# Scoring by halves of tokens in one loop, x1's rows behind up, and down's last 64 rows loaded early

## The chip, the cores and the metric

The kernel runs on one NeuronCore of a Trainium2 chip. The metric is device time of one execution in microseconds, lower is better.

## The reference

One decode step (one token, width D = 640) of a transformer block with adaptive layer norm. All tensors are bf16.

```python
mod = silu(c) @ w_mod                       # 640 -> 6 x 640: sa, ca, ga, sb, cb, gb
h = layernorm(x) * (1 + ca) + sa
q = h @ wq                                  # 32 heads of 128
scores = q . k_cache * 128 ** -0.5          # k_cache, v_cache: [32, 16384, 128]
o = softmax(scores) @ v_cache               # per head
x = x + ga * (o @ wo)                       # wo: 4096 x 640
h = layernorm(x) * (1 + cb) + sb
x = x + gb * ((silu(h @ w_gate) * (h @ w_up)) @ w_down)   # 640 -> 1728 -> 640
```

There are 32 key and value heads for 32 query heads, so each cached row is used once. K and V together are 268 MB, the weights some 22 MB; all of it is read in one execution.

## The kernel before

**Pairs.** The 32 heads are handled in NP = 16 pairs. A pair's K lies in one of two slots of `kring` as [128 partitions, 256 tokens, 128 elements]: partitions 0 to 63 hold one head, 64 to 127 the other, and each partition has 256 tokens, 64 KB. V goes to the one buffer `vbuf` in the same shape, V of the last pair to slot 0 of `kring`. Before the pairs these buffers hold `w_mod` and `wq`, after them `wo` (in `vbuf`) and the MLP's weights (in slot 1).

**Score of a pair.** DVE multiplies K by the query in place and adds halves of the element axis onto each other ("folds"); TensorE (PE) sums the 16 elements that are left by 16 matmuls with an identity into `S_ps`. This is done in two parts per pair. In the loop `score(p, c)` takes a half of the elements for all 256 tokens: one multiplication (L554), two folds (L559, L564), and `reduce_mm` (L544) adds its 16 matmuls of 256 columns to the same sum; the two parts together give the 16 + 16 elements. For the first and the last pair `score_end(p, c)` takes all 128 elements of a half of the tokens (128): one multiplication (L570), three folds (L576), and `reduce_end` (L584) runs 16 matmuls of 128 columns.

**Softmax and PV.** `largest(p)` takes the largest score (DVE, L590), spreads it on a diagonal (ACT, `d2`, L592) and shares it over the partitions by a matmul (L594). `weigh(p)` takes the least over the row (DVE, L598) and makes the exponentials (ACT, L602). `pv(p)` is 64 matmuls of 512 columns (L518) and a copy by ACT (`acc`, L524); `diag(p)` picks the wanted blocks by eight matmuls (L533) and a copy by ACT (`ot`, L537).

**Order.** Every engine runs its own list in the order in which the Python code calls `op`; an operation waits on semaphores of the operations in `deps` on other engines. `step(p)` calls: score part 0 of p (with `largest(p-1)` and `weigh(p-1)` between its steps), reduction, `pv(p-1)`, score part 1, reduction, `diag(p-1)`. `plan.in_loop` turns the pairs into a hardware loop: PE from pair 1 to 14, one pair per turn; ACT and DVE from pair FIRST = 3 to 14, two pairs per turn. Addresses and the values waited for are then computed from the turn. SP's list, the DMA issues, is written out. The last pair (PL = 15) stands behind the loops in an order of its own: first part, `pv(14)`, `diag(14)`, second part, then `largest(15)` and `weigh(15)`.

**DMA.** SP issues K of pair p+1 when the last reduction of pair p-1 is done, V of pair p when `pv(p-1)` is done, `wo` after `pv(14)`, and after the last reduction `w_gate`, `w_up` and five pieces of `w_down`. All run in the one queue of SP. Only c and x are loaded from ACT's queue.

**Tail.** After `pv(15)` and `diag(15)`: `on`, `z`, `am`, `as` (normalizing, and bringing the output vector into columns), the projection (L684), `wo_row` and `wo_cols` (L690, L696), x1 (L706), the second layer norm, `gate0` and `gate` (L721), `x1_rows` (L743: x1 spread to four strips of rows by eight matmuls), `up` (L721), the SiLU steps on DVE and ACT (L750 to L755), `gu` (L756), and `down` (L773), where each of the four strips of 32 partitions makes a quarter of the 640 outputs. 1728 is 13 x 128 + 64: gate and up take the last 64 columns in a 14th chunk that overlaps the 13th by 64. Their down rows are loaded as 128 half rows of 640 B, so a matmul with `twice` (L757) doubles each value onto two partitions, and `gu_half` (L759) masks by parity.

The lines that the change touches, from the kernel:

Of the kernel before, what the change touches and what calls it, by code (L numbers as in the profile page):

```python
# [218 lines left out]
def build(nc, A_x, A_k, A_v, A_wq, A_wo, B_wg, B_wu, B_wd, c_in, w_mod, out):  # L219
# [15 lines left out]
    DOWN = [(0, 0, 4), (1, 0, 4), (2, 0, 4), (None, 0, 0), (3, 0, 1)]  # L235
    FCH = NF + 1
    QW = 32
    QR = 16
    RW = D // 4
    FIRST = 3  # L240

    es = ExitStack()
    with es:
# [20 lines left out]
        wt_v = kb[:, wd0 + NF * D:wd0 + NF * D + D // 2]  # L264
# [15 lines left out]
        rows = qbc[0:1].rearrange("p a d -> p (a d)")[:, 0:2 * D].rearrange("p (j n) -> p j n", j=2)  # L280
# [33 lines left out]
        gu_half = sb("gu_half", [128, 2], BF16)  # L314
        even = sb("even", [128, 2], F32)
        twice = sb("twice", [128, 64, 2], BF16)
# [3 lines left out]
        x1_sp = acc_sb[:, 0:RW]  # L320
        q_f = qbc[:].rearrange("p a d -> p (a d)")
# [32 lines left out]
        d_c = dma(rows[:, 0, :], c_in, "c", name="dma_c", eng="act")  # L354
        d_x = dma(rows[:, 1, :], A_x[0], "x", name="dma_x", eng="act")
# [18 lines left out]
        def f_cx(e):  # L374
            last = None
            for j in range(2):
                for k in range(KC):
                    last = e.matmul(cx_ps[:, j * KC + k:j * KC + k + 1], lhsT=rows[0:1, j, k:D:KC],
                                    rhs=ones_bf[0:1, 0:1], start=True, stop=True)
            return last  # L380
        o_cx = op(PE, f_cx, deps=[d_c, d_x, o_onesb], name="cx_col")
        o_cc = op(ACT, lambda e: e.activation(out=c_col[:], in_=cx_ps[:, 0:KC], func=ACTF.Copy), deps=[o_cx], name="c_f32")
        o_ec = op(ACT, lambda e: e.activation(out=ec[:], in_=c_col[:], func=ACTF.Exp, scale=-1.0), deps=[o_cc], name="ec")
        o_xf = op(ACT, lambda e: e.activation(out=x_f32[:], in_=cx_ps[:, KC:2 * KC], func=ACTF.Copy, accum_out=st[:, 0:1]), deps=[o_cx], name="x_f32")
# [35 lines left out]
        def f_e32(e):  # L420
# [3 lines left out]
        o_even = op(DVE, lambda e: e.tensor_reduce(  # L424
            out=even[:], in_=ident[:].rearrange("p (j k) -> p k j", k=2), axis=AX.X, op=ALU.add), deps=[o_ident], name="even")
        o_twice = op(DVE, lambda e: e.tensor_copy(out=twice[64:128], in_=ident[64:128, 64:128].unsqueeze(2).broadcast_to([64, 64, 2])), deps=[o_ident], name="twice")
# [44 lines left out]
        for g in range(H // 4):  # L471
            b = g % 2

            def f_q(e, g=g, b=b):
                last = None
                for k in range(KC):
                    last = e.matmul(q_ps[b][:, 0:512], lhsT=h_col[:, k:k + 1].broadcast_to([128, 128]),  # L477
                                    rhs=wq_v[:, k, g * 512:(g + 1) * 512], start=(k == 0), stop=(k == KC - 1))
                return last
# [8 lines left out]
            o_qev.append(ev)  # L488

# [50 lines left out]
        def reduce_mm(p, c, fold):  # L540
            def f_R(e):
                last = None
                for d in range(QW * c, QW * c + QR):
                    last = e.matmul(S_ps[:, 0:T2], lhsT=ident[:], rhs=kring[:, bass.ds(plan.slot(p), 1), :, d].rearrange("p o t -> p (o t)"),  # L544
                                    start=(d == 0), stop=(d == QW + QR - 1))
                return last
            return op(PE, f_R, deps=[fold, o_ident, o_exp[p - 1], o_gb, o_m1], name="R%d_%d" % (p, c))

        def score(p, c, between=None):

            kv4 = kring[:, p % 2].rearrange("p t (a d) -> p t a d", a=2)[:, :, :, QW * c:QW * c + QW]
            def f_mult(e):
                q4 = qbc[:, bass.ds(plan.at(p), 1), :].rearrange("p o (a d) -> p o a d", a=2)[:, :, :, QW * c:QW * c + QW].broadcast_to([128, T2, 2, QW])
                return e.tensor_tensor(out=kv4, in0=kv4, in1=q4, op=ALU.mult)  # L554
            o_m = op(DVE, f_mult,
                     deps=[d_k[p][-1]] + o_qev[p // 2], name="mult%d_%d" % (p, c))
            if between:
                between[0]()
            o_f = op(DVE, lambda e: e.tensor_tensor(out=kv4[:, :, 0], in0=kv4[:, :, 0], in1=kv4[:, :, 1], op=ALU.add),  # L559
                     deps=[o_m], name="fold%d_%d" % (p, c))  # L560
            if between:
                between[1]()
            lo = kv4[:, :, 0]
            return op(DVE, lambda e: e.tensor_tensor(out=lo[:, :, 0:QR], in0=lo[:, :, 0:QR], in1=lo[:, :, QR:QW], op=ALU.add),  # L564
                      deps=[o_f], name="fold%d_%db" % (p, c))

        def score_end(p, c, between=None):

            kv = kring[:, p % 2, KCUT[c]:KCUT[c + 1]]
            o = op(DVE, lambda e: e.tensor_tensor(  # L570
                out=kv, in0=kv, in1=qbc[:, p, :].unsqueeze(1).broadcast_to([128, KCUT[c + 1] - KCUT[c], 128]), op=ALU.mult),
                deps=[d_k[p][min(c, len(d_k[p]) - 1)]] + o_qev[p // 2], name="mult%d_%d" % (p, c))
            for i, w in enumerate((64, 32, 16)):
                if between and i < 2:
                    between[i]()
                o = op(DVE, lambda e, w=w: e.tensor_tensor(out=kv[:, :, 0:w], in0=kv[:, :, 0:w], in1=kv[:, :, w:2 * w], op=ALU.add),  # L576
                       deps=[o], name="fold%d_%d_%d" % (p, c, w))
            return o

        def reduce_end(p, c, fold):  # L580
            def f_R(e):
                last = None
                for d in range(16):
                    last = e.matmul(S_ps[:, KCUT[c]:KCUT[c + 1]], lhsT=ident[:], rhs=kring[:, p % 2, KCUT[c]:KCUT[c + 1], d],  # L584
                                    start=(d == 0), stop=(d == 15))
                return last
            return op(PE, f_R, deps=[fold, o_ident, o_exp[p - 1] if p else o_gb], name="R%d_%d" % (p, c))
# [22 lines left out]
        def step(p):  # L610
            reduce_mm(p, 0, score(p, 0, before(p)))
            pv(p - 1)
            o_R[p] = reduce_mm(p, 1, score(p, 1))
            diag(p - 1)

# [3 lines left out]
        reduce_end(0, 0, score_end(0, 0))  # L619
        o_R[0] = reduce_end(0, 1, score_end(0, 1))  # L620
        NLOOP = NP - 2
        for p in range(1, NP - 1):
            plan.in_loop(("pe",), "pairs", p - 1, NLOOP)
            if p >= FIRST:
                plan.in_loop(("act", "dve"), "pairs", (p - FIRST) // 2, (NP - 1 - FIRST) // 2)
            load_k(p + 1)
            step(p)
            load_v(p)
        plan.out_of_loop(("pe", "act", "dve"))

        PL = NP - 1
        load_v(PL)
        f0 = score_end(PL, 0, before(PL))
        reduce_end(PL, 0, f0)
        pv(PL - 1)
# [3 lines left out]
        diag(PL - 1)  # L641
        f1 = score_end(PL, 1)
        o_R[PL] = reduce_end(PL, 1, f1)
# [10 lines left out]
        for i, (b, r0, r1) in enumerate(DOWN):  # L654
            if b is None:
                dst, src = wt_v, B_wd[NF * 128:F, :].rearrange("q (h n) -> (q h) n", h=2)
            else:
                f0, n, j0 = BLOCKS[b]
                dst, src = wd_v[:, j0 + r0:j0 + r1, :], B_wd[f0:f0 + 128 * n, :].rearrange("(p r) n -> p r n", r=n)[:, r0:r1, :]
# [12 lines left out]
            in1=on_f[:].unsqueeze(2).broadcast_to([128, H, 4]), op=ALU.mult), deps=[o_on, o_msk], name="z")  # L672
        o_am = op(PE, lambda e: e.matmul(A_ps[:, 0:H], lhsT=Z[:], rhs=e32[:], start=True, stop=True),
# [14 lines left out]
        for c in range(len(WCUT) - 1):  # L688
            o_p = project(c)
        o_wr = [op(ACT, lambda e, a=a, b=b, ps=ps: e.activation(out=wo_row[:, a:b], in_=ps[:, 0:b - a], func=ACTF.Copy),  # L690
                   deps=[o_p, f1], name="wo_row%d" % a) for ps, a, b in ((wr_ps[0], 0, 512), (wr_ps[1], 512, D))]
# [18 lines left out]
        def chunk(j):  # L710
            if j == NF:

                return slice(F - 128, F)
# [3 lines left out]
        def f_gu(e, wv, ps_t, src, n, k0, k1):  # L717
            last = None
            for k in range(k0, k1):
                for j in range(FCH):  # L720
                    last = e.matmul(ps_t[:, n * j:n * j + n], lhsT=wv[:, k, chunk(j)], rhs=src[:, n * k:n * k + n],  # L721
                                    start=(k == 0 and j == 0), stop=(k == KC - 1 and j == FCH - 1), skip_group_check=True)
# [17 lines left out]
        def f_xr(e):  # L740
            last = None
            for r in range(4):
                last = e.matmul(xr_ps[32 * r:32 * r + 32, 0:RW], lhsT=wide(msk[:, r:r + 1]), rhs=x1_sp, start=True, stop=True,  # L743
                                tile_position=(0, 32 * r))
            return last
        o_xr = op(PE, f_xr, deps=[o_xsp, o_ot[PL], o_msk], name="x1_rows")
        o_x1r = op(ACT, lambda e: e.activation(out=x1_row, in_=xr_ps[:, 0:RW], func=ACTF.Copy), deps=[o_xr], name="x1_row")
# [83 lines left out]
```

## Time and profile before

| What | us |
|---|---|
| median of 3 runs | 680.36 |
| the runs | 680.29, 680.36, 680.75 |
| the profiled execution's own time | 680.16 |
| its span, first to last instruction | 678.4 |
| DVE busy in it | 512.9 (76%) |
| PE busy in it | 362.4 (53%) |
| ACT busy in it | 46.8 (7%) |
| bytes read | 290.47 MB, 428 GB/s over the span |

The profile is of one execution, and its times count from the span's first instruction. PE is TensorE's matmul part and PEld its weight loads, DVE VectorE, ACT ScalarE, SP SyncE. A row of the chain of waits is "start, duration, what"; a row of the timeline is "start, duration, engine, line, operation, tiles, count" and, in brackets, how long the engine sat idle before it and what ended that. A row of windows has the stretch, its length, the busy time of PE, PEld, DVE, ACT and POOL with the number of instructions, the granted clock of PE as a share of full speed, the DMA engines' busy share and GB/s.

### The profile page before, as it was taken

The page shows a single profiled execution, that of the slowest core. Times are in us where ns is not written, and L with a number is a line of the kernel's source. Part 1 is how long each engine was busy: PE and PEld are TensorE (multiplying, and loading weights), DVE is VectorE, ACT ScalarE, POOL GpSimd, SP SyncE. Part 2 cuts the span into 40 slices and gives each one's busy share as a digit, 9 for nine tenths or more (in the row PEclk, how much of TensorE's full clock was granted, in tenths as well). Part 3 has the DMA queues.
Part 4 walks back from the last instruction along what each step waited for, and adds up shares of the span by engine and source line. Part 5 has one row for each costly group of instructions (what it writes and reads, how often), then busy time and mean ns, then how long its engine had stood idle before and what let it go on. Part 6 is the DMA issues. An engine that isn't in the chain of part 4 may idle for free.

```text
span 678.4 us, 5422 instructions
## 1 busy us (share of the span) xinstructions
PE 362.4 (53%) x2075; PEld 145.4 (21%) x2076; DVE 512.9 (76%) x184; ACT 46.8 (7%) x147; POOL 0.7 (0%) x6
## 2 busy tenths in 40 slices
PE   2522275755628174654818365572817465481677
PEld 1101122221212122221302122121212222130236
DVE  2189997959596996959597795959698695959802
ACT  1110000100000000000000010000000000000011
POOL 0000000000000000000000000000000000000000
PEclk9965565565756565565657565565757555575666
DMA  9999999999999999999999999999999999999997
GB/s 374 439 459 437 433 433 430 429 429 433 433 433 433 433 433 437 433 433 433 433 433 433 437 433 433 433 433 433 433 433 433 433 433 433 433 433 433 430 409 305
DMA packets 6355, 290.58 MB, mean 428 GB/s; under 512 B 714, under 2 KB 972, under 8 KB 1484
## 3 DMA queue, kind: packets, MB, share of 16 engines
q1 hardware_dynamic: 6340, 290.48, 99.2%
q8 instruction: 5, 0.08, 0.0%
q14 instruction: 2, 0.02, 0.0%
q10 hardware_dynamic: 8, 0.00, 0.0%
HBM read 290.47 MB, written 0.00 MB: 428 GB/s over the span
## 4 chain that ended last, share of the span: by engine, by line
DMA 43%; DVE 30%; issue 13%; PE 13%; ACT 1%; DVEq 0%; SPq 0%
DMA kring<-in_A_k_cache_dram 40%; DVE kring L554 10%; PE psb L544 7%; DVE kring L559 6%; DVE kring L570 5%; DVE kring L576 5%; DMA vbuf<-in_A_wq_dram 4%; DVE kring L564 3%; PE psb L477 1%; PE psb L518 1%; PE psb L721 1%; PE psb L684 1%; PE psb L584 1%; PE psb L696 0%; DVE pm L590 0%
## 5 line engine op out<-in xcount | busy, mean ns | idle before, releaser
L554 DVE TENSOR_TENSOR kring<-kring,qbc 128x16384 bf16<-128x16384 bf16 x28 | 243.3, 8688 | 96.2 <-DMA kring<-in_A_k_cache_dram 96.2
L544 PE MATMUL psb<-kring,ident 128*128 x448 | 197.5, 607 | 122.4 <-DVE kring L564 122.4
L559 DVE TENSOR_TENSOR kring<-kring 128x8192 bf16<-128x8192 bf16 x28 | 123.8, 4421 | 0.5
L544 PEld LDWEIGHTS psb<-kring,ident 128*128 128x128 bf16 x448 | 53.9, 120 | 250.2 <-issue 249.3
L518 PE MATMUL psb<-vbuf,PZ 128*8 128x512 bf16 x960 | 79.9, 506 | 0.0
L594 PE MATMUL psb<-d,bd_f 128*128 128x64 f32 x32 | 11.0, 446 | 122.0 <-ACT d L592 122.0
L564 DVE TENSOR_TENSOR kring<-kring 128x4096 bf16<-128x4096 bf16 x28 | 64.0, 2287 | 0.5
L570 DVE TENSOR_TENSOR kring<-kring,qbc 128x16384 bf16<-128x16384 bf16 x4 | 34.8, 8689 | 23.4 <-ACT qbc L484 16.0
L518 PEld LDWEIGHTS psb<-vbuf,PZ 128*8 128x8 bf16 x960 | 26.4, 107 | 58.1 <-issue 47.7
L584 PE MATMUL psb<-kring,ident 128*128 128x128 bf16 x64 | 14.5, 392 | 41.3 <-DVE kring L576 41.3
L594 PEld LDWEIGHTS psb<-d,bd_f 128*128 128x128 f32 x32 | 8.0, 311 | 124.1 <-DVE pm L590 114.5
L576 DVE TENSOR_TENSOR kring<-kring 128x8192 bf16<-128x8192 bf16 (+2 forms) x12 | 31.7, 2646 | 0.3
L533 PEld LDWEIGHTS psb<-sel,acc_sb 128*128 128x128 f32 x128 | 28.5, 310 | 8.4 <-issue 4.3
L533 PE MATMUL psb<-sel,acc_sb 128*128 128x2 f32 x128 | 25.6, 322 | 1.4 <-ACT acc_sb L524 1.4
L524 ACT ACTIVATE acc_sb<-psb 128x512 f32<-128x512 f32 x16 | 9.6, 597 | 209.7 <-PE psb L518 209.7
L602 ACT ACTIVATE PZ<-psb,nb 64x256 bf16<-64x256 f32 x32 | 15.0, 469 | 64.8 <-DVE nb L598 64.6
L584 PEld LDWEIGHTS psb<-kring,ident 128*128 128x128 bf16 x64 | 7.4, 121 | 47.7 <-DVE kring L576 42.5
L592 ACT ACTIVATE d<-negid,pm 128x64 f32<-128x64 f32 x16 | 5.6, 348 | 154.9 <-DVE pm L590 154.9
L477 PE MATMUL psb<-vbuf,h_col 128*128 128x512 bf16 x39 | 9.9, 421 | 8.3 <-DMA vbuf<-in_A_wq_dram 8.3
L537 ACT ACTIVATE OT_sb<-psb 128x2 f32 (+1 forms) x16 | 2.8, 172 | 154.3 <-PE psb L533 154.3
L590 DVE TENSOR_REDUCE pm<-psb 128x1 f32<-128x256 f32 x16 | 6.7, 418 | 3.7 <-PE psb L584 3.7
L477 PEld LDWEIGHTS psb<-vbuf,h_col 128*128 128x128 bf16 x40 | 4.0, 108 | 14.7 <-DMA vbuf<-in_A_wq_dram 8.8
(103 smaller groups left out, 80.2 us busy)
## 6 DMA issues: line engine op xcount, KB each, us to landing
kring<-in_A_k_cache_dram SPq DMA_DIRECT2D x2, 4096.0 KB, 40.1
vbuf<-in_A_wq_dram SPq DMA_DIRECT2D x1, 5120.0 KB, 25.8
kring<-in_w_mod_dram SPq DMA_DIRECT2D x1, 4800.0 KB, 14.1
vbuf<-in_A_wo_dram SPq DMA_DIRECT2D x1, 4480.0 KB, 22.6
kring<-in_B_w_gate_dram SPq DMA_DIRECT2D x1, 2160.0 KB, 18.9
kring<-in_B_w_up_dram SPq DMA_DIRECT2D x1, 2160.0 KB, 23.5
kring<-in_B_w_down_dram SPq DMA_DIRECT2D x3, 640.0 KB, 25.7
vbuf<-in_A_wo_dram SPq DMA_DIRECT2D x1, 640.0 KB, 23.8
```

What stands on the lines that cost most here:

```text
L477: last = e.matmul(q_ps[b][:, 0:512], lhsT=h_col[:, k:k + 1].broadcast_to([128, 128]), rhs=wq_v[:, k, g * 512:(g + 1) * 512], start=(k == 0 ...
L518: last = e.matmul(acc_ps[32 * s:32 * s + 8, :], lhsT=PZ[:, j, :], rhs=v_at(p)[:, 4 * j:4 * j + 4, :].rearrange("p t d -> p (t d)"), start= ...
L533: last = e.matmul(OT_ps[:, 0:2], lhsT=acc_sb[:, 128 * i:128 * (i + 1)], rhs=sel[:, i:8:4], start=(i == 0), stop=(i == 3))
L544: last = e.matmul(S_ps[:, 0:T2], lhsT=ident[:], rhs=kring[:, bass.ds(plan.slot(p), 1), :, d].rearrange("p o t -> p (o t)"), start=(d == 0) ...
L554: return e.tensor_tensor(out=kv4, in0=kv4, in1=q4, op=ALU.mult)
L559: o_f = op(DVE, lambda e: e.tensor_tensor(out=kv4[:, :, 0], in0=kv4[:, :, 0], in1=kv4[:, :, 1], op=ALU.add), deps=[o_m], name="fold%d_%d" ...
L564: return op(DVE, lambda e: e.tensor_tensor(out=lo[:, :, 0:QR], in0=lo[:, :, 0:QR], in1=lo[:, :, QR:QW], op=ALU.add), deps=[o_f], name="fol ...
L570: o = op(DVE, lambda e: e.tensor_tensor(out=kv, in0=kv, in1=qbc[:, p, :].unsqueeze(1).broadcast_to([128, KCUT[c + 1] - KCUT[c], 128]), op= ...
L576: o = op(DVE, lambda e, w=w: e.tensor_tensor(out=kv[:, :, 0:w], in0=kv[:, :, 0:w], in1=kv[:, :, w:2 * w], op=ALU.add), deps=[o], name="fol ...
L584: last = e.matmul(S_ps[:, KCUT[c]:KCUT[c + 1]], lhsT=ident[:], rhs=kring[:, p % 2, KCUT[c]:KCUT[c + 1], d], start=(d == 0), stop=(d == 15))
L594: o_mx[p] = op(PE, lambda e: e.matmul(mx_ps[:, 0:64], lhsT=bd_f[:], rhs=d2[:], start=True, stop=True), deps=[o_d2, o_bd1, o_bd2, o_nb[p - ...
L602: o_exp[p] = op(ACT, lambda e, half=half, ps=ps: e.activation(out=PZ[ps, :, 4 * half:4 * half + 4], in_=S_ps[ps, 0:T2].rearrange("p (c i) ...
```

## The change

1. `score` and `reduce` replace the two forms of each. All pairs are scored by halves of tokens: part c multiplies all 128 elements of 128 tokens and folds three times; a reduction of 16 matmuls takes 128 columns. Pair 0 has one reduction of 256 columns after both parts.
2. The last pair moves into the loops: PE from pair 1 to 15, ACT and DVE from FIRST = 2 to 15. V of pair 15 is issued ahead of its step as before; `diag(14)` now stands where `step` has it, behind the second reduction.
3. The query matmuls (8 groups of 5) run in a PE loop of four turns.
4. c and x are loaded to partitions 0 and 1 of one tile and brought into columns by 5 matmuls instead of 10.
5. `x1_rows` becomes one matmul with a 128-column tile `strips` (made on DVE behind `z`) in place of eight with 32 columns, and stands behind `up`.
6. gate and up treat the last 64 columns as three short chunks (`SHORT`) of 32 + n columns, n = 16, 12 and 4, at the end of their lists; the 14th chunk goes.
7. down's last 64 rows go to a tile `wt` of their own, set to zero by GpSimd at the start. They are loaded by `load_short` in 24 loads: at pairs 4 to 7, after V, six each, of 4, 3 or 1 rows on every fourth partition. Their load at the end goes, and with it `twice`, `gu_half` and `even`. `gu` is made by one multiplication for 13 chunks and six small ones, and `down_short` is 12 matmuls between the second and the third piece of down.

```diff
-    DOWN = [(0, 0, 4), (1, 0, 4), (2, 0, 4), (None, 0, 0), (3, 0, 1)]
-    FCH = NF + 1
+    DOWN = [(0, 0, 4), (1, 0, 4), (2, 0, 4), (3, 0, 1)]
+    SHORT = [(0, 16), (16, 12), (28, 4)]
+    NS = len(SHORT)
+    KT = 48
+    FCH = NF + NS
+    DEALT = 4
-    FIRST = 3
+    FIRST = 2
...
+        wt = sb("wt", [KT, NS, D], BF16)
...
+            for k in range(KC):
+                last = e.matmul(cx_ps[:, 2 * k:2 * k + 2], lhsT=rows[:, k:D:KC], rhs=ident[0:2, 0:2], start=True, stop=True)
...
+            plan.in_loop(("pe",), "queries", g // 2, H // 8)
...
         def score(p, c, between=None):
...
+            kv = kring[:, p % 2, KCUT[c]:KCUT[c + 1]]
+
             def f_mult(e):
...
+                return e.tensor_tensor(out=kv, in0=kv, in1=qbc[:, bass.ds(plan.at(p), 1), :].broadcast_to([128, KCUT[c + 1] - KCUT[c], 128]), op=ALU.mult)
+            o = op(DVE, f_mult, deps=[d_k[p][min(c, len(d_k[p]) - 1)]] + o_qev[p // 2], name="mult%d_%d" % (p, c))
+            for i, w in enumerate((64, 32, QR)):
...
+        def reduce(p, a, b, fold):
             def f_R(e):
                 last = None
+                for d in range(QR):
+                    last = e.matmul(S_ps[:, a:b], lhsT=ident[:],
+                                    rhs=kring[:, bass.ds(plan.slot(p), 1), a:b, d].rearrange("p o t -> p (o t)"),
+                                    start=(d == 0), stop=(d == QR - 1))
...
         def step(p):
-            reduce_mm(p, 0, score(p, 0, before(p)))
+            reduce(p, 0, T2 // 2, score(p, 0, before(p)))
             pv(p - 1)
-            o_R[p] = reduce_mm(p, 1, score(p, 1))
+            o_R[p] = reduce(p, T2 // 2, T2, score(p, 1))
             diag(p - 1)
+        PL = NP - 1
+        def load_short(at):
+            last = None
+            for j, (f0, n) in enumerate(SHORT):
+                for a in (0, 32):
+                    f = 128 * NF + f0 + a
+                    last = dma(wt[a + at:a + n:4, j, :], B_wd[f + at:f + n:4, :], "wt", deps=[o_wtz], name="dma_wt%d_%d_%d" % (j, a, at))
+            return last
...
-        reduce_end(0, 0, score_end(0, 0))
-        o_R[0] = reduce_end(0, 1, score_end(0, 1))
-        NLOOP = NP - 2
-        for p in range(1, NP - 1):
-            plan.in_loop(("pe",), "pairs", p - 1, NLOOP)
+        score(0, 0)
+        o_R[0] = reduce(0, 0, T2, score(0, 1))
+        for p in range(1, NP):
+            plan.in_loop(("pe",), "pairs", p - 1, NP - 1)
             if p >= FIRST:
-                plan.in_loop(("act", "dve"), "pairs", (p - FIRST) // 2, (NP - 1 - FIRST) // 2)
-            load_k(p + 1)
-            step(p)
-            load_v(p)
+                plan.in_loop(("act", "dve"), "pairs", (p - FIRST) // 2, (NP - FIRST) // 2)
+            if p < PL:
+                load_k(p + 1)
+                step(p)
+                load_v(p)
+                if DEALT <= p < DEALT + 4:
+                    d_wt = load_short(p - DEALT)
+            else:
+                load_v(p)
+                step(p)
         plan.out_of_loop(("pe", "act", "dve"))
-        PL = NP - 1
-        load_v(PL)
-        f0 = score_end(PL, 0, before(PL))
-        reduce_end(PL, 0, f0)
-        pv(PL - 1)
...
-        diag(PL - 1)
-        f1 = score_end(PL, 1)
-        o_R[PL] = reduce_end(PL, 1, f1)
         largest(PL)
         weigh(PL)
...
+        o_strips = op(DVE, lambda e: e.tensor_copy(
+            out=strips.rearrange("p (j k) -> p j k", k=32), in_=msk[:].unsqueeze(2).broadcast_to([128, 4, 32])), deps=[o_msk, o_diag[PL]], name="strips")
...
+            for k, j in [(k, j) for k in range(k0, k1) for j in range(NF)] + [(k, j) for k in range(KC if k1 == KC else 0) for j in range(NF, FCH)]:
+                w = 128 if j < NF else 32 + SHORT[j - NF][1]
+                last = e.matmul(ps_t[0:w, n * j:n * j + n], lhsT=wv[:, k, chunk(j)], rhs=src[:, n * k:n * k + n],
...
+        o_xr = op(PE, lambda e: e.matmul(xr_ps[:, 0:RW], lhsT=strips, rhs=x1_sp, start=True, stop=True),
+                  deps=[o_xsp, o_ot[PL], o_strips], name="x1_rows")
...
+        o_gum = scale_up("gu", 0, 128, 0, NF)
+        o_gus = [scale_up("gu%d_%d" % (a, j0), a, a + n, j0, j0 + 1) for a in (0, 32) for j0, (f0, n) in enumerate(SHORT, NF)]
...
+            short = [(gu_col[0:KT, NF + j:NF + j + 1], wt[:, j, RW * r:RW * r + RW], r) for j in range(NS) for r in range(4)]
...
+            if i == 2:
+                op(PE, lambda e, work=short: f_down(e, 1, work), deps=o_gus + [d_wt], name="down_short")
+            prev = op(PE, f_down, deps=[o_gum, d_wd[i], o_nb[PL]], name="down%d" % i)
```

## The prediction, made before the changed kernel ran

> **What bounds the kernel now.** I read the page's rows by slices first, then the chain of waits in order of time, then the timeline around the last pair, the tail in windows of the granted clock, and the DMA issues.
>
> ```profile
> DMA  9999999999999999999999999999999999999997
> GB/s 374 439 459 437 433 433 430 429 429 433 433 433 433 433 433 437 433 433 433 433 433 433 437 433 433 433 433 433 433 433 433 433 433 433 433 433 433 430 409 305
> ```
>
> The 16 DMA engines are full and move 433 GB/s until the last slice. In the loop nothing but the bytes counts: K of a pair lands every 38.70 us (the 16.8 MB of a pair at 433 GB/s), whatever the engines do in between, as long as each transfer is issued before the one ahead of it ends. Only the end is different. The chain of waits there:
>
> ```profile
> 570.08 38.72 DMA kring<-in_A_k_cache_dram
> 608.83 8.69 DVE kring L570
> ...
> 642.44 0.05 issue
> 642.48 3.65 PE psb L584 x16
> 646.15 0.43 DVE pm L590
> 646.61 0.36 ACT d L592
> ...
> 670.51 0.69 PE psb L743 x8
> 671.20 2.37 PE psb L721 x70
> ...
> 673.89 0.18 PE psb L757
> 674.08 2.02 PE psb L773 x50
> ```
>
> From the landing of the last K (608.80 us) to the output a single file of small steps runs, 69.6 us long, with no wait for a DMA in it. But the stream is close behind. The five down loads were issued 0.475 us apart from 646.99 on, so the fourth and fifth went out at 648.41 and 648.89:
>
> ```profile
> kring<-in_B_w_down_dram SPq DMA_DIRECT2D x1, 160.0 KB, 26.5
> kring<-in_B_w_down_dram SPq DMA_DIRECT2D x1, 80.0 KB, 26.6
> ```
>
> They land at 675.0 and 675.4; the last matmuls on them start at about 675.7. So the tail has two bounds 0.3 us apart: what is added to the file costs its full price, what is taken from it brings 0.3 us at most.
>
> **The loop: nothing.** Each score half is now all 128 elements of 128 tokens. That is a multiplication of 8.69 us as before (128x16384 at L554 and at L570 alike), then folds of 4.42, 2.29 and 1.23 us (the L576 forms) instead of 4.42 and 2.29: DVE +2 x 1.23 = +2.45 us a pair. The reduction's 16 matmuls are 128 columns wide, 3.65 us at L584 against 7.07 at L544. K's slot is released after two scores and one reduction: +2.45 - 3.42 = -1.0 us; V's, after one of each and PV, at +1.2 - 3.4 = -2.2 us. Both earlier. DVE waited 7.4 us a pair for K (L554: 96.2 us in 13 waits) and still has 4.9. If that cover were gone, every pair would pay up to 2.45 us, 34 us in 14 pairs. Pair 0 now has one reduction of 7.07 us at the end instead of 3.65, so K of pair 2 is issued at 77.3 instead of 73.9; V of pair 0 lands at 86.2 (105.5, when that K landed, less 19.35 for its bytes), so 8.9 us of cover are left. The query loop and the new c/x transposition end long before: the first K half lands at 36.8.
>
> **The 24 loads: +0.2 us (0 to 1.5).** They go to SP's queue behind V of pairs 4 to 7, six each, before the next K issue. Six issues at 0.43 to 0.475 us are 2.9 us of SP, and SP waits some 10 us for that K's slot. A row of 1280 B is a packet of 55 ns in the trace (c, x and the 160 KB load), and an 80 KB load of 128 rows landed 0.2 us after the one before it. 64 rows over 16 engines are 64 x 0.055 / 16 = 0.22 us; all 24 loads beginning on one engine, as c and x were one packet each, make 24 x 0.055 = 1.3 us there, 1.5 with their semaphore writes. V of pair 15 ended on the engines between 645.5 and 647.0, so a leading engine can lose 1.2 us unseen, and the one that carried c and x led by that. I take 0.2. [...]
>
> **Pair 15 inside the loop: +0.3 us.**
>
> ```profile
> 563.00 7.05 PE L544 MATMUL psb<-kring,ident 128*128 x16 [2.32 <-DVE kring L564]
> 569.87 1.68 PE L533 MATMUL psb<-sel,acc_sb 128*128 128x2 f32 x8
> 570.34 8.69 DVE L554 TENSOR_TENSOR kring<-kring,qbc 128x16384 bf16<-128x16384 bf16 x1 [7.48 <-DMA kring<-in_A_k_cache_dram]
> 608.83 8.69 DVE L570 TENSOR_TENSOR kring<-kring,qbc 128x16384 bf16<-128x16384 bf16 x1 [7.41 <-DMA kring<-in_A_k_cache_dram]
> ```
>
> K of pair 14, in the loop, landed at 570.11 and its multiplication began 0.23 us later; that of pair 15, after the loop, 0.03 later (its landing is 570.08 + 38.72). Address and wait arithmetic costs 0.2 us here, and 0.09 once more where the reduction waits (0.13 us of issue in the loop, 0.05 after it). Bounds 0.2 to 0.5, if leaving the three loops costs something the trace doesn't show.
>
> **diag(14) behind the last reduction: +1.35 us (0.8 to 1.5).** In the old ending diag(14), its eight matmuls and ACT's copy ot14 stood before the last score and were hidden by it. In step() they stand behind the second reduction, on PE and on ACT, ahead of largest(15): ACT cannot copy d2 of pair 15 before ot14, and ot14 needs diag(14). From the timeline: the last reduction matmul begins at 645.74 and d2 at 646.61, 0.87 later. With diag behind it PE needs 0.22 until the first diag matmul, 1.68 for the eight (the L533 row above), 0.11 until ot14, 0.2 until d2: 2.2 us. Difference 1.35; 0.8 if PE is at full clock (1.05 for eight, the 656.61 step). In the loop the same order costs nothing, since the next K isn't there yet. Nothing hides it here.
>
> **The MLP: +0.4 us (-0.3 to +1.5).** Three short chunks of 48, 44 and 36 columns for five k are 15 matmuls instead of 5, for gate and up each. 70 took 2.37 us, 34 ns each; the 32-column ones of L773 36.5. At 40 ns, a little above both since changing widths may cost something: 15 x 40 - 5 x 34 = +0.43 each, +0.86; with 60 ns +1.5. Behind up, the x1_rows matmuls leave PE free for up 0.69 us earlier. They are now one fp32 product of two passes with 0.26 us between starts (the L594 pairs), 0.55 us of PE, while DVE makes gu (0.09 + 0.18) and PE would have waited anyway; before, gu, twice_gu and down stood 0.6 us behind up's last matmul too, so this is even: -0.69 in all. The six small scale_up multiplications, 0.2 us each, end 1.7 us behind up and down_short needs them at 1.8, behind 32 down matmuls; uncovered they cost up to 1.2. Down has 52 + 12 = 64 matmuls instead of 56, 8 x 36.5 ns = +0.29. Together 0.86 - 0.69 + 0.29 = +0.46, less 0.05 for DVE steps now beside up: 0.4.
>
> **Sum.** 0.2 + 0.3 + 1.35 + 0.4 = 2.25 us. The profiled execution took 680.16 us (span 678.4); 682.4. That execution is the fastest shown, 0.2 below the median 680.36, so the forecast is 2.0 us above the median.
>
> **Rivals.** *The clock falls better (not slower).*
>
> ```profile
> 648.07:651.48 3.41, 2.29 (x22) 1.09 (x26) 0.36 (x1) 1.05 (x4) 0.00 (x0) 0.50 1.12 483
> 651.48:654.90 3.42, 3.42 (x40) 1.12 (x36) 0.00 (x0) 0.00 (x0) 0.00 (x0) 0.50 0.95 409
> 654.90:658.31 3.41, 2.05 (x28) 1.21 (x20) 0.31 (x2) 0.77 (x2) 0.00 (x0) 1.00 0.91 381
> ```
>
> The column before the last two is the granted clock, PE's busy time stands first. The clock changes on a grid of 3.41 us, and the last PV, begun at 649.8, ran 5.1 of its 6.1 us at half clock, because the first full window on it ended only at 654.9. If the tail moves by 1.6 us, PV begins at 651.4, on a boundary: 3.5 us at half clock, the other 3.3 in 1.7: 1.0 us back. If the projection L684 also keeps its full-clock share, another 0.4: 681.0. Against it: at 659.8 the projection would fill only 1.9 us of its window and could lose 0.6 (683.0). Where on the grid the tail will fall can't be told before the run, so I count neither into the sum. 0.18. [...]
>
> *The stream's end decides (no change).* If diag(14) ran beside the d2 chain, the MLP's parts would nearly cancel and the down loads at 675.4 would set the end: 680.0 to 680.4. It decides from a shift of the file under 0.3 us on. Against: the order on ACT. 0.06.
>
> *Small loads stop the stream.* If the engines idle during the 24 issues, 24 x 0.43 = 10 us: 692. For the 80 KB load they didn't. 0.04. [...]
>
> *Short matmuls don't pipeline.* At the full 0.17 us of one (L721) 30 of them add 30 x 0.17 - 10 x 0.034 = 4.8 instead of 0.86 us: 686.3. L743 and L757 switch widths without that. 0.06.
>
> **Numbers.** My forecast has 0.66. Deviations of its terms, taken as independent: upward 1.3 (loads), 0.2, 0.2, 1.1, 0.6 (clock), 1.8 together; downward 0.2, 0.1, 0.55, 0.7, 1.4, 1.7 together: 680.7 to 684.2, which also holds the first rival. A measurement of this kernel can tell about 0.2%, 1.4 us: no change means 679.0 to 681.7. Slower by more: most of the forecast, the two dear rivals and a little of the first, 0.75. Faster by more is nearly shut out, since the stream's end holds the kernel at 679.8 or more: 0.02. Rest 0.23.
>
> **What would show it.** The K landings stay 38.70 us apart and the last one comes within 0.5 us of 608.8; DVE's wait for K falls to about 5 us a pair; between the last reduction and d2 of pair 15 stand eight L533 matmuls and the L537 copy, 2.2 us from the last reduction matmul to d2; gate and up have 80 matmuls each, down follows up by 0.6 us. I am wrong if the last K lands more than 1.5 us late, if d2 follows the reduction by 0.9 us, or if a wait for a DMA appears behind 650 us.

## The result

| | before | changed |
|---|---|---|
| median of 21 runs each, us | 680.27 | 681.55 |
| lowest and highest, us | 679.75, 680.79 | 680.77, 684.13 |
| profiled execution, us | 680.16 | 681.07 |
| its span, us | 678.4 | 679.1 |

The changed kernel is slower: its median is 1.3 us higher, and the ratio over all runs, which also feels the slowest ones, is 1.0026 (95% interval 1.0019 to 1.0033), 1.8 us. Its runs fall into two groups: a lower one of 14 from 680.8 to 682.3 and an upper one of 7 from 683.1 to 684.1, while the kernel before stays within 1.0 us (1.0 to 1.6 us in the later comparisons). Why there are two groups is the larger half of the story.

The profile after was taken of a run of the lower group. The rows by slices on its page say that the stream is as full as before:

```profile
DMA  9999999999999999999999999999999999999996
GB/s 379 436 463 432 432 429 432 433 432 433 432 432 432 432 430 436 430 432 434 432 433 433 432 432 432 432 432 432 432 436 432 436 432 432 432 432 432 437 418 276
```

Its chain of waits, in order of time, from the last reduction on (L559 is the reduction, L534 diag, L568 d2, L519 PV, L665 the projection, L702 gate and up, L729 x1_rows, L747 down):

```profile
642.79 0.13 issue
642.92 3.63 PE psb L559 x16
646.55 1.51 PE psb L534 x8
...
648.36 0.36 ACT d L568
...
651.57 5.16 PE psb L519 x61
...
659.82 2.41 PE psb L665 x64
...
668.16 5.21 PE psb L702 x147
673.37 0.83 PE psb L729 x2
674.20 2.52 PE psb L747 x38
```

diag(14) now stands between the reduction and d2, as the prediction had it. But PV and the projection take less than before, where their rows are:

```profile
649.82 6.12 PE psb L518 x64
...
659.04 3.71 PE psb L684 x64
```

The changed kernel's PV, begun at 651.5, ran at half clock (0.51 granted from 651.4 to 654.8) to 654.7 only (before, at 0.50, from 649.8 to 654.9), and its projection at full clock throughout; before, the projection, begun at 659.0, ran at half clock (0.50) to 661.7. The windows of the changed kernel show it, in the column before the last two:

```profile
654.80:658.20 3.40, 2.69 (x43) 1.44 (x36) 0.00 (x0) 0.60 (x1) 0.00 (x0) 1.00 0.84 350
658.20:661.60 3.40, 2.23 (x56) 1.43 (x59) 0.62 (x3) 0.37 (x2) 0.00 (x0) 1.00 1.02 436
```

What the tail lost at d2 it got back there, and then lost again in the MLP. Start of the first matmul to end of the last, from the timelines of both:

| Step of the tail, us | before | changed | difference |
|---|---|---|---|
| last K lands | 608.80 | 609.03 | +0.23 |
| landing to the last reduction | 33.68 | 33.89 | +0.21 |
| last reduction's start to d2's | 4.13 | 5.44 | +1.31 |
| PV of pair 15 | 6.15 | 5.19 | -0.96 |
| projection | 3.66 | 2.37 | -1.29 |
| gate's start to down's end | 8.39 | 9.54 | +1.15 |

The sum is +0.65, the last down matmul ends 0.63 later (676.69 against 676.06), and the time is 0.91 longer; 0.21 of that lies between span and time.

### The profile page after: what moved, and what is told of

Its sections match the earlier page's. It is cut to its first block, busy times and chain, and to the rows that moved or that the text cites. A ratio compares the mean times of both kernels' runs of the same rounds, so it can differ in the third digit from the quotient of the medians.

```text
span 679.1 us, 5625 instructions
## 1 busy us (share of the span) xinstructions
PE 265.9 (39%) x2076; PEld 143.5 (21%) x2076; DVE 547.2 (81%) x216; ACT 46.9 (7%) x147; POOL 2.4 (0%) x8
## 4 chain that ended last, share of the span: by engine, by line
DMA 46%; DVE 32%; issue 14%; PE 8%; ACT 0%; DVEq 0%; SPq 0%; ACTq 0%
DMA kring<-in_A_k_cache_dram 46%; DVE kring L551 17%; DVE kring L546 14%; PE psb L559 4%; PE psb L702 1%; PE psb L519 1%; PE psb L534 0%; PE psb L747 0%; PE psb L665 0%; PE psb L677 0%; DVE nb L574 0%; DVE pm L566 0%; ACT PZ L578 0%; PE psb L729 0%; SPq L90 0%
## 5 line engine op out<-in xcount | busy, mean ns | idle before, releaser
L546 DVE TENSOR_TENSOR kring<-kring,qbc 128x16384 bf16<-128x16384 bf16 x32 | 278.0, 8688 | 84.9 <-DMA kring<-in_A_k_cache_dram 84.9
L551 DVE TENSOR_TENSOR kring<-kring 128x8192 bf16<-128x8192 bf16 (+2 forms) x96 | 253.8, 2644 | 2.3
L559 PE MATMUL psb<-kring,ident 128*128 (+1 forms) x496 | 116.1, 400 | 252.3 <-DVE kring L551 252.3
L559 PEld LDWEIGHTS psb<-kring,ident 128*128 128x128 bf16 x496 | 59.4, 120 | 304.4 <-issue 234.5
L519 PE MATMUL psb<-vbuf,PZ 128*8 128x512 bf16 x960 | 79.2, 502 | 0.0
L519 PEld LDWEIGHTS psb<-vbuf,PZ 128*8 128x8 bf16 x960 | 26.2, 106 | 51.6 <-issue 40.9
L534 PEld LDWEIGHTS psb<-sel,acc_sb 128*128 128x128 f32 x128 | 28.1, 319 | 2.6 <-ACT acc_sb L525 1.2
L534 PE MATMUL psb<-sel,acc_sb 128*128 128x2 f32 x128 | 26.2, 327 | 0.7 <-ACT acc_sb L525 0.7
L568 ACT ACTIVATE d<-negid,pm 128x64 f32<-128x64 f32 x16 | 5.6, 348 | 158.3 <-DVE pm L566 158.3
L477 PE MATMUL psb<-vbuf,h_col 128*128 x40 | 10.6, 422 | 8.2 <-DMA vbuf<-in_A_wq_dram 8.1
L484 ACT ACTIVATE qbc<-psb 64x256 bf16<-64x256 f32 x16 | 6.1, 378 | 11.8 <-PE psb L477 11.6
L437 PE MATMUL psb<-kring,silu_c 128*32 128x480 bf16 x40 | 4.2, 604 | 4.9 <-DMA kring<-in_w_mod_dram 4.9
L578 ACT ACTIVATION_READ_ACCUMULATOR PZ<-psb,nb (+1 forms) x32 | 6.0, 188 | 0.0
L574 DVE TENSOR_REDUCE nb<-psb 128x1 f32<-128x64 f32 x16 | 3.5, 218 | 2.5 <-PE psb L570 2.5
```

What stands on the lines that cost most here:

```text
L484: ev.append(op(ACT, lambda e, g=g, b=b, half=half, ps=ps: e.activation(out=qbc[ps, 2 * g:2 * g + 2, :], in_=q_ps[b][ps, :].rearrange("p (a ...
L519: last = e.matmul(acc_ps[32 * s:32 * s + 8, :], lhsT=PZ[:, j, :], rhs=v_at(p)[:, 4 * j:4 * j + 4, :].rearrange("p t d -> p (t d)"), start= ...
L534: last = e.matmul(OT_ps[:, 0:2], lhsT=acc_sb[:, 128 * i:128 * (i + 1)], rhs=sel[:, i:8:4], start=(i == 0), stop=(i == 3))
L546: return e.tensor_tensor(out=kv, in0=kv, in1=qbc[:, bass.ds(plan.at(p), 1), :].broadcast_to([128, KCUT[c + 1] - KCUT[c], 128]), op=ALU.mult)
L559: last = e.matmul(S_ps[:, a:b], lhsT=ident[:], rhs=kring[:, bass.ds(plan.slot(p), 1), a:b, d].rearrange("p o t -> p (o t)"), start=(d == 0 ...
L578: o_exp[p] = op(ACT, lambda e, half=half, ps=ps: e.activation(out=PZ[ps, :, 4 * half:4 * half + 4], in_=S_ps[ps, 0:T2].rearrange("p (c i) ...
```

## The experiments

Each comparison is with the kernel before, run beside it on the same chip. "Lower" and "upper" group are the two groups of times above. A kind clock is one that gives the last PV and the projection more full clock, as in the profile above.

**diag first.** In `step`, on every pair:

```diff
-            o_R[p] = reduce(p, T2 // 2, T2, score(p, 1))
-            diag(p - 1)
+            last_fold = score(p, 1)
+            diag(p - 1)
+            o_R[p] = reduce(p, T2 // 2, T2, last_fold)
```

> The changed kernel with diag(p-1) put ahead of the second reduction in step(), on every pair. Theory (diag and ot14 held up d2): from the first matmul of the last reduction to d2 4.1 us, as before the change, not the 5.4 of the changed kernel; time 0.8 to 1.3 us below the changed kernel, about 680.3 to 680.8. Rival (the small loads or the MLP cost it all, and d2 was hidden): d2 comes earlier but the time stays at 681.5.

Measured: 681.08 us (680.75 to 682.65), ratio 1.0015 (1.0006 to 1.0024). From the last reduction to d2 it is 4.12 us again: this is what held d2. The time did not follow. The median is 0.5 us below the changed kernel's 681.55, not 0.8 to 1.3, and 2.5 below the 683.61 of the changed kernel run again on the same chip (below): medians of two groups differ by how many runs fall into each. At equal clock the two profiled runs, both with full clock for about 10 us from the middle of PV on, took the same, 681.09 and 681.07 us. The chain says where the 1.3 us went:

```profile
647.03 23.26 DMA kring<-in_B_w_up_dram
670.29 0.14 issue
670.43 2.92 PE psb L703 x80
673.35 0.83 PE psb L730 x2
674.18 2.52 PE psb L748 x53
```

The gate was done at 669.32, and up had to wait for its weights, which land at 670.29. From up's start at 670.43 it is 6.3 us to the end of down, so this kernel cannot end its down before 676.7, whatever the steps ahead do. The changed kernel's up started at 670.43 as well, 0.21 after its weights: with a kind clock it runs into the same bound, and the later d2 is hidden there. Before, the up weights landed at 670.05, up started at 671.14, and 4.9 us of work followed: the wait was not there, and the last down load at 675.4 was the next bound.

**The kernel before with diag(14) late.**

```diff
-        diag(PL - 1)
         f1 = score_end(PL, 1)
         o_R[PL] = reduce_end(PL, 1, f1)
+        diag(PL - 1)
```

> The kernel before, with diag(14) moved behind the last reduction and nothing else. Theory: d2 1.3 us later (5.4 us from the first matmul of the last reduction), time 0.5 to 1.3 us above before, since the granted clock may give a part back: 680.8 to 681.6. Rival (a move on PE is covered by the stream's end): within 0.2 us of before, 680.3.

Measured: 680.36 us (679.95 to 682.61), ratio 1.0011 (1.0002 to 1.0019). Seven runs lie from 679.95 to 680.47, five from 681.24 to 682.61. The median is the rival's, the five upper runs are the theory's. In the profiled run, of 679.97, d2 comes 5.36 us after the reduction's start, 1.23 later than before, and PV and the projection take 5.07 and 2.37 us. Its chain ends in the wait for a down load that lands at 674.84, so with this kind clock the later d2 cost nothing. This one line, moved alone, makes both groups. That the five slower runs are those with an unkind clock, in which the tail's own length counts, fits, but none of them was profiled.

**No small loads**: the last 64 rows of down are left out of the result.

```diff
-                if DEALT <= p < DEALT + 4:
-                    d_wt = load_short(p - DEALT)
```

> The changed kernel without its 24 small loads (the last 64 rows of down are taken as zero). Theory A (the loads cost 0.2 us at the last K's landing; the runs at 683 to 684 come from the clock in the tail): last K lands at 608.8 instead of 609.0, median 681.3, runs above 683 still there. Theory B (the loads make the runs at 683 to 684 by falling on an engine that is already late): K lands at 608.8, the runs above 683 are gone and the spread is under 1.5 us.

Measured: 681.19 us (680.21 to 683.63), ratio 1.0024 (1.0012 to 1.0036); four of ten runs in the upper group. So the loads do not make the groups. The last K lands at 609.13, 0.10 later than with the loads, but this end hides where the lag arose. Without the loads K of pair 2 already lands at 106.01, 0.48 later than in the kernel before (105.53), and from there each K lands 38.70 us after the one before it. In the changed kernel it lands at 105.80, and the step is 38.70 again but for one: the first K behind the last six loads comes 0.11 late (338.00, then 376.81). In its repetition below the steps in the stretch of the loads are 0.35 late in all, in the other six profiles with the 24 loads 0 to 0.27. So the loads do cost the stream 0 to 0.35 us, and 0.11 of the 0.23 are theirs; the rest was there before the first of them. In the packets, an instruction fetch of 16 KB stops one DMA engine for 1.08 us at 91.9; in the kernel before one does so for 1.0 us at 106.0. Whether that makes the rest is not settled.

**The changed kernel again**, unchanged.

> The changed kernel unchanged, for a second profile beside the others on the same chip. If the clock in the tail makes the spread: the profile's time follows the tail's share of full clock, about 681 with PV of pair 15 and the projection at 5.2 and 2.4 us, about 683 with some 6 and 4 us, with the last K landing at 609.0 in both. If the loads make it: the last K lands 1 us or more later in an execution of 683.

Measured: 683.61 us (680.83 to 684.29); eight of twelve runs in the upper group, and the profile is of one of these, 683.55 us. Its chain:

```profile
646.65 1.51 PE psb L534 x8
...
651.67 6.08 PE psb L519 x63
...
660.86 3.70 PE psb L665 x64
...
670.48 5.22 PE psb L702 x147
675.70 0.83 PE psb L729 x2
676.53 2.52 PE psb L747 x50
```

Against the lower run's chain only two lines differ by more than 0.1 us: PV 6.08 against 5.16 and the projection 3.70 against 2.41, together 2.2 of the 2.5 us. The last K landed at 609.12, 0.09 later. In the trace the granted clock was full from 654.7 to 665.0 in the lower run; in the upper only from 656.7 to 660.1 and from 663.5 to 666.9. In the same windows as above the upper run has

```profile
654.80:658.20 3.40, 2.92 (x36) 0.85 (x28) 0.00 (x0) 0.42 (x1) 0.00 (x0) 0.72 0.85 351
658.20:661.60 3.40, 2.00 (x21) 1.49 (x25) 0.62 (x3) 0.54 (x3) 0.00 (x0) 0.78 1.03 440
```

These four changes lie 3.4 us apart, and all changes in the profiles of before and of the lower run whole steps of 3.41 us. This grid lay 2.0 us later under the same work. What a step of the grid must hold to keep the clock does not come out as one number: with 2.07 us of PE work (656.7 to 660.1) the clock fell behind it, in the lower run it stayed behind 2.69 and 2.23, and it fell behind 2.46 in the profile of "No down_short".

**Idle matmuls ahead of PV.**

```diff
+        busy(1)     # matmuls of 512 columns into a bank that nothing reads
         largest(PL)
+        busy(3)
         weigh(PL)
```

> The changed kernel with four idle matmuls of 512 columns on PE, one ahead of the last largest() and three behind its matmul, into a bank that nothing reads, to fill the clock's window ahead of PV. Theory (the runs at 683 to 684 are those in which PV and the projection fall on a half-clock window): runs above 683 become rare, fewer than 2 of 12 where they were about half, median 681.2. Rival (they have another cause): as many as without, each 0.2 us longer.

Measured: 681.26 us (681.04 to 681.63, 11 runs), ratio 1.0017 (1.0008 to 1.0026). Not one of the 11 runs is in the upper group, where the changed kernel had 15 of 33. That was on another chip than the repetition, but on it the upper group is there without idle matmuls, in four of ten runs of "No down_short" and four of five of "x1_rows ahead". In its own profile the clock is full from 654.9 only, and PV takes 5.27 us, like the lower group without idle matmuls; what they do where the grid lies badly was not profiled. With five of them the clock was full ahead of PV in the profile of "Both and five idle matmuls": 3.14 us of PE work between 645.9 and 649.3, and full clock from 649.3, before PV begins at 650.0. With the repetition this settles the spread: it is the clock that PV and the projection meet. In the three profiled runs at 683 to 684 the projection takes 3.70 to 4.51 us, in every profiled run of a lower group 2.4.

**x1_rows ahead of up again**, the new single product:

```diff
+        o_xr = op(PE, ...)     # x1_rows and its copy, as changed
         o_u = op(PE, lambda e: f_gu(e, wu_v, u_ps, h2_col, 1, 0, KC), ...)
-        o_xr = op(PE, ...)
```

> The changed kernel with x1_rows put back ahead of up and nothing else. Theory: where the granted clock is kind up waits for its weights (landed 670.2), and x1_rows fits ahead of it: 680.3 to 680.7 there instead of 681.1; where it isn't, nothing waits for a load and only the 0.25 us are saved by which x1_rows held down up: 683.2 to 683.9. Rival (behind up is the better place, as the prediction had it): 0.7 us slower than the changed kernel in both.

Measured: 683.68 us (681.82 to 684.03, five runs), ratio 1.0053 (1.0039 to 1.0067), four in the upper group. In its profile, of the one lower run, gate's start to down's end takes 9.82 us against 9.54: behind up is the better place where nothing waits, by 0.28 us and not the 0.69 of the prediction. Here down follows up's end by 0.32 us, against 0.76 with x1_rows between them: behind up the product holds down by 0.44. My own expectation of a gain was wrong in both groups; in the lower run up started 1.2 us after its weights had landed.

**Both, diag first and x1_rows ahead.**

> The changed kernel with diag ahead of the second reduction and with x1_rows put back ahead of up. Theory (in e1_diag_first the gate was done at 669.3, up had to wait for its weights until 670.3, and what stands behind up, 6.2 us to the last down matmul, set the end): x1_rows goes into that wait, down starts 0.25 to 0.8 us earlier, then waits for its last load at 675.4; time 680.2 to 680.5, like before, 0.6 to 0.9 us under e1. Rival (x1_rows costs the same on either side): 681.1.

Measured: 680.93 us (680.35 to 682.93), ratio 1.0020 (1.0011 to 1.0030). Six runs lie from 680.35 to 680.93 and five from 682.3 to 682.9. Where up waits for its weights (in the profile until 670.15), x1_rows costs nothing ahead of it: the lower group begins 0.4 us under that of diag first (680.35 against 680.75). The upper group stays, so it was wrong to expect the spread of before.

**No down_short**: the 12 matmuls on down's last 64 rows are left out, the loads and small multiplications stay.

> The changed kernel without the 12 matmuls of down_short (the last 64 rows of down are left out); the 24 loads and the six small multiplications stay. If a short matmul costs what a down matmul does (12 x 37 ns): from the first down matmul to the last 0.45 us less, 2.1 us. If changing the row width empties PE's pipeline on both sides, 0.25 us each: 0.95 us less, 1.6 us, unless the last down load at 675.3 holds it.

Measured: 680.80 us (680.32 to 683.44), ratio 1.0017 (1.0005 to 1.0029). From the first down matmul's start to the last one's end 1.92 us against 2.56: 0.64 less, 0.44 for the 12 themselves at 37 ns each and 0.20 more, less than the 0.5 expected for two changes of width.

**The kernel before with five idle matmuls** (`busy(2)` and `busy(3)` in the same places).

> The kernel before with five idle matmuls of 512 columns, two behind the last reduction and three behind the last largest(). Theory (PV and the projection of the tail get full clock, and the stream's end then bounds the tail): up starts when its weights land, about 670.1, the last down matmuls wait for 675.4; 679.7 to 680.0, 0.2 to 0.5 us under before, with a spread under 0.6 us. Rival (the file of the tail has no slack to give, since it was bound by the stream already): 680.2, the same as before.

Measured: 680.08 us (679.84 to 680.19), against 680.26 of before beside it, ratio 0.9996 (0.9987 to 1.0005): not told apart. The spread is 0.35 us instead of 1.5. Its chain ends in the stream:

```profile
648.02 26.77 DMA kring<-in_B_w_down_dram
674.79 0.04 issue
674.84 1.02 PE psb L782 x21
```

With full clock from 653.1 to 663.4 its gate is done at 668.55 and x1_rows at 669.24, it waits for the up weights until 670.1 and for a down load until 674.8. This is why before spreads less than the changed kernel: a kind clock runs into the stream's end 0.3 us further on.

**Both and five idle matmuls.**

> e5_diag_first_x1_ahead with the same five idle matmuls. Theory: its runs at 682 to 683 go, what is left is the length of the MLP behind the landing of up's weights, 680.4 to 680.5, 0.2 to 0.3 us above before. Rival: the runs at 682 to 683 stay.

Measured: 681.03 us (680.36 to 682.30), ratio 1.0013 (1.0004 to 1.0022). Five of the eleven runs still lie from 681.6 to 682.3. The profile, of the run at 682.30, shows an outcome that neither side had:

```profile
634.80 23.60 DMA vbuf<-in_A_wo_dram
658.40 0.14 issue
658.54 4.50 PE psb L675 x64
```

PV met full clock from its start and took 3.63 us, the projection was ready early, and its weights landed only at 658.40. The clock went back to half at 656.1, PE stood from 656.5 to 658.5, and the projection took 4.50 us, nearly all at half clock. It ended at 663.04, against 662.23 in the changed kernel's profile: a step made faster ran into the next transfer, and what it had won was lost and more. How much of that the wait did and how much the clock is open; in "No down_short" the projection took 4.51 us at half clock without a wait.

**One row a load**, 64 loads in place of 24.

> The changed kernel with the 64 rows in 64 loads of one row each, 16 at each of the pairs 4 to 7, in place of 24 loads. If a load of one row always goes to the same DMA engine: 64 x 55 ns = 3.5 us there, less the 1.2 to 1.7 us by which another engine is late already, so the last K lands about 2 us later, at 611, and the time rises by 2 us. If rows are spread: 609.1. If each load costs 0.01 us outside the span (1.73 us there with no load, 1.95 to 2.13 with 24): 2.3 to 2.6 us between time and span.

Measured: 687.51 us (687.25 to 689.84), ratio 1.0117 (1.0101 to 1.0133). The last K lands at 615.42, 6.3 us later than with 24 loads. One engine ended its last V packet at 653.67, all others by 648.14. Each row is one packet, and only one engine is late, so all rows went to the same one. The price was over twice the expected one. The first K behind each batch of 16 rows comes 0.09, 1.77, 2.16 and 2.13 us late: the first batch is almost hidden by an engine that was later already, and a full price of 2.13 to 2.16 is some 0.13 us a row, not 0.055. In the packets a batch takes 1.2 us, and the 64 KB packet behind it 3.39 us instead of 2.42. Time less span is 1.73 us, so the number of loads does not set that.

**Six loads** of neighbouring rows at pair 4.

> The changed kernel with the 64 rows in six loads of 16, 12 and 4 rows on neighbouring partitions at pair 4, in place of 24. If the number of loads costs time outside the span: 1.75 to 1.85 us between time and span, 0.2 us below the changed kernel; if it is the tile or the bytes: 1.95 to 2.13 as with 24. Last K at 609.0 to 609.1 either way.

Measured: 681.66 us (681.07 to 684.14), ratio 1.0031 (1.0020 to 1.0042). The last K lands at 609.55, 0.5 later than expected; the first K behind the six loads comes 0.65 late, so six loads in one pair are no better than 24 in four. Time less span is 1.74 us. It was 1.73 or 1.74 in every profile of before, without loads, with 64 and with six, and 1.95 to 2.13 in all eight with the 24 loads on every fourth partition. That those loads cost 0.2 to 0.4 us outside the span is what the profiles suggest, but six of the changed kernel's 21 runs have only 1.7 to 1.8. When they cost it, and how, is open.

## Why the prediction was right or wrong

The forecast of slower held, and 681.55 lies in the range, 0.9 us under the 682.4. It held narrowly: the prediction put no change at 679.0 to 681.7, so its 0.75 was for times above that, and the median lies 0.15 inside; only the interval of the ratio, 1.0019 to 1.0033, tells the two kernels apart. That the median came so near the sum is luck: the sum has two errors of opposite sign, an MLP that was sized too small and a clock that gave back more than was allowed for, and the same program run again had a median of 683.61.

- **The loop.** Right. K lands every 38.70 us (570.33, 609.03), and DVE's wait for K at L546 is 5.0 to 5.2 us in each pair from 3 on, where 4.9 had been worked out. The 2.45 us of DVE did not reach the stream.
- **The 24 loads, +0.2.** The landing moved by 0.23, but only 0.11 of that came with the loads, and 0 to 0.35 in the eight profiles that have them. That the stream hardly feels it when a few engines lose time was read right: four engines end V of pair 15 some 1 to 2 us behind most others (646.35 to 647.28, against 645.1 to 645.7), almost hidden behind an engine that was late already (647.20). What they may cost outside the span the sum did not have.
- **Pair 15 in the loop, +0.3.** 0.21.
- **diag behind the reduction, +1.35.** 1.31, and 1.23 alone in the old kernel. The step was read right, and so was the order on ACT. That nothing hides it was wrong for a kind clock: there the wait for up's weights hides it, since diag first ends down at 676.70 and the changed kernel at 676.69.
- **The MLP, +0.4.** This is the term that was mis-sized: 1.15. From the two timelines: gate and up took 1.01 us longer for their short chunks (0.86 expected); moving x1_rows took 0.69 off before up, but down's first matmul now follows up's end by 0.76 us instead of 0.45, so that part was not even, as the prediction took it: the two passes of 160 columns in fp32 hold PE for 0.83 us, not for the 0.55 taken from passes of 64 columns; down itself takes 0.51 us more, not 0.29. The pieces add to 1.01 - 0.69 + 0.31 + 0.51 = 1.14.
- **The sum.** In the upper run of the repetition PV and the projection take what they took before (6.12 and 3.64 us), so the clock drops out: 683.55 against 680.16, +3.4 us. Forecast at the same clock were 2.25. Of the 1.1 us between, 0.75 are the MLP and 0.34 time outside the span (2.08 against 1.74). At a kind clock the change costs 1.2 us: 681.07 against 679.91 in the profile of the kernel before with idle matmuls.
- **The clock rival, 0.18.** It was not a rival but a draw made in every run. It gave back 2.25 us in the profiled run (0.96 + 1.29), more than the 1.4 allowed. About half of the runs get it (18 of 33), which puts this median under the forecast.
- **The stream's end.** The prediction let the stream hold the kernel at 679.8. For the changed kernel it holds a us later, because up's weights, and not the last down load, are what the longer MLP waits for; diag first showed the wait. It was missing from the list of bounds.

## What to carry to other kernels

Before moving the last turn of a loop back into the loop, read what the hand-written ending had put in another order: an operation that is free in every other turn can stand on the path in the last one. When a file of short steps runs beside a full stream, give each transfer that it meets its own line (landing, and the work that must follow it), since the bound may change from the last load to an earlier one. And where a tail depends on a clock that changes under it (here on a grid of 3.41 us), compare by equal clock, run by run, before a median is explained.

## What was not expected of the hardware

The same program differs by up to 3.4 us (680.77 to 684.13), and 2.2 of the 2.5 us between two profiled runs lie in two bursts of matmuls, by where the clock's grid of 3.41 us falls under them. With four idle matmuls ahead of PV none of 11 runs was in the upper group. Full clock early need not pay: in one profile PV took 3.63 us, then the clock fell, the load was late, and the projection took 4.50 us where 2.37 were seen. And in "One row a load" each row cost its engine about 0.13 us, while its packet took 0.055: half of that showed only in the next 64 KB packet, which took 3.39 us instead of 2.42.
